# Top-k attention with a squared-ReLU layer on one core: the order of the last two batches, the place of the V casts, and the end of the program

## The chip, the core and the metric

One of the eight cores of a Trainium2 chip runs the whole program. The core has TensorE (PE in the profile, with its weight loads as PEld), VectorE (DVE), ScalarE (ACT), GpSimd (POOL) and SyncE (SP), each with an instruction queue of its own that it works off in order; waits between them go by semaphores. The metric is the device time of one execution in microseconds (us), and a kernel's time is the median of its runs.

## The reference

Attention over 8 batches of 8 heads, 576 rows of 64, in which each row keeps only its 32 largest scores; then a layer with a squared ReLU over the 4608 tokens.

```python
scores = scale * np.matmul(q, k.transpose(0, 1, 3, 2))
kth = np.partition(scores, -top_k, axis=-1)[..., -top_k:-top_k + 1]
scores = np.where(scores >= kth, scores, -1000000000.0)
attn = softmax(scores)                       # top_k = 32
x = np.matmul(attn, v)                       # tokens x 512, heads side by side
h = np.maximum(x @ w_in, 0.0)                # 512 -> 2048
out = h * h @ w_out                          # 2048 -> 512
```

## The kernel before

**Steps.** Two heads of a batch form a pair, so there are 32 pairs, four to a batch. A head's 576 rows are four chunks of 128 and a rest of 64. One step takes two blocks of 128 rows by 576 scores: chunk c of both heads of a pair, or the rests of two pairs. The list `steps` (L224 to L231) has 18 steps a batch, U = 144 in all, numbered u. In each batch the first pair does its four chunks, then come the rests of the first two pairs, then the other three pairs go chunk by chunk in turn, with the rests of the last two pairs behind chunk 0. A chunk of the tokens (`x_tok`) is complete when all four pairs have done it, so the four chunks of a batch are complete at its steps 7, 11, 14 and 17, counted from 0.

**One step on the engines.** TensorE makes the scores of step u+1 into two PSUM tiles, `sc_a` and `sc_b` (L254), and ScalarE copies them to `s` (L257). VectorE takes pairwise maxima (`pairs_of`, L273 and L274; `quads_of`, L282 and L283) and finds the 32 largest values in four rounds of MAX8 and MATCH_REPLACE8 (`topk`, L333 and L337). ScalarE's "far copy" (`copy_far`, L289) brings one half of the maxima from PSUM to `most`, which GpSimd (`lesser`, L307) and L282 of the next step read. ScalarE negates the ends of the top-k (`negate`, L352); GpSimd marks what is to be dropped (`drop`, L369), and a DMA with accumulation (L373) takes it off `s`. Two steps later ScalarE takes the exponentials (`exps`, L377) and SP starts a DMA transpose to `wT` (`turn`, L386). TensorE multiplies `wT` with V (`products`, `weigh`, L412) into `av`, one PSUM tile for all steps; VectorE inverts the sums (`invert`, L417) and ScalarE writes the scaled result into `x_tok` or, for rests, `x_rem` (`place`, L433 and L440). `finish` is `invert` and `place`. A step's products are taken `back` = 3 steps later and finished a step after that; from u = Z = U - 5 on `back` is 2.

**Preparing a pair.** `prep_units` has four parts: the transposes of q and of k (`main`, ScalarE's copy L162), those of the rests (`rest`, L199, L200, L202), and the casts of V (`values`, L206 and twice L209). `prepare` runs one part a step (two before step 8), between the exponentials and the far copy; `due` says when a pair is begun, and if a pair isn't ready when its scores are to be made, a loop ahead of `scores` runs what is missing. Its ten loads go three a step through SP's queue (`fetch`).

**The layer.** Two complete chunks (in the last batch one) make a block: `x_unit` turns them, with a DMA transpose (L477) or on TensorE (L470, the last batch's chunks 1 to 3, which wait in the list `moves`), and the rests of two batches make a block in the same way (`rem_unit`, L483, L489). A block is eight "up" pieces (four for one chunk with half the rows each: L514, then ReLU L519 and square L525 on ScalarE, or L523 on VectorE once `late` is set), and four "down" pieces a chunk (L537, over 16 matmuls in one PSUM bank `dn_ps`), then a copy (L542) and a store (L544). One chunk of 128 rows in the last batch is thus four up and four down pieces of about the same work. `piece` takes one from either list in turn; `dense(u, x)` runs, for x = 0 and x = 1, one piece each, or two each in the last 14 steps (L582), and filler matmuls (L553) if there is none. With `later`, what ScalarE does after a piece is put off to the next step (`behind`).

**The end.** Three blocks of the last two steps are masked on VectorE (L381) instead of being dropped by DMA, and the last two steps' weights are turned on TensorE (`turn_by_tensor`, L397, copies L399 and L401). Three more rounds of the loop, u = U to U + 2, do this together with products, pieces and `finish`; the pieces that are left follow in a last loop (L744). An up piece's PSUM tile is one of two `gen` buffers, in the last rounds sometimes `sc_a` or `sc_b` (L508). If a flag shows that the fast way did not separate the 32 largest values, a general version runs behind; it takes no part in the times here.

Of the kernel before, what the change touches and what calls it, by code (L numbers as in the profile page):

```python
# [23 lines left out]
def kernel(  # L24
# [192 lines left out]
    def whole(i):  # L217
        return [((i, c, 0), (i, c, 1)) for c in range(4)]
# [5 lines left out]
    steps = []  # L224
    for b in range(B):
        p0 = 4 * b
        steps += whole(p0) + rests(p0)
        for c in range(4):
            steps += [((i, c, 0), (i, c, 1)) for i in range(p0 + 1, p0 + 4)]
            if c == 0:  # L230
                steps += rests(p0 + 2)  # L231
    U = len(steps)
    first = {}
# [153 lines left out]
        st[u]["wT"] = wT  # L387


    def turn_by_tensor(u, x):  # L390
        if x == 0:
            st[u]["wT"] = scp.tile([128, 9, 128], bf16, name="wT", bufs=3)
            st[u]["tp"] = ps_sc.tile([128, 2, 1024], bf16, name="sc_" + "ab"[u - U + 2])
        flat = w_two[u % 3][:, :, :].rearrange("p x n -> p (x n)")
        tp = st[u]["tp"][:, x, 0:512 + 128 * x].rearrange("p (n r) -> p n r", r=128)
        for n in range(4 + x):
            pin(nc.tensor.transpose(tp[:, n, :], flat[:, (4 * x + n) * 128:(4 * x + n + 1) * 128], id_h[:, :]))  # L397
        if x == 0:
            pin(nc.vector.tensor_copy(st[u]["wT"][:, 0:4, :], tp))  # L399
        else:  # L400
            pin(nc.scalar.activation(st[u]["wT"][:, 4:9, :], tp, AF.Copy))  # L401

    def weigh(u, x):
        i, c, a = steps[u][x]
        va, wT = prep[i][3], st[u]["wT"]
        o = av[:, x, :]
        for g in range(2 if c == 4 else 1):
            rows = slice(64 * g, 64 * g + 64) if c == 4 else slice(0, 128)
            h = g if c == 4 else a
            for n in range(5):  # L410
                block_of, chunk = (5 * x + n, n) if n < 4 else (4, 4 + x)
                pin(nc.tensor.matmul(out=o[rows], lhsT=wT[:, block_of, rows], rhs=va[:, chunk, h, :], start=(n == 0), stop=(n == 4)))  # L412
        av_left[i] -= 1

    def invert(u):
        r = small.tile([128, 2, 1], f32, name="rsum", bufs=4)
        pin(nc.vector.reciprocal(r[:, :, :], av[:, :, 64:65]))  # L417
        st[u]["r"] = r

    x_tok = {}  # L420
# [4 lines left out]
    def place(u):  # L425
        for x, (i, c, a) in enumerate(steps[u]):
            b, pr = pairs[i]
            o, r = av[:, x, :], st[u]["r"]
            if c < 4:
                if (b, c) not in x_tok:  # L430
                    x_tok[b, c] = ffp.tile([128, 512], bf16, name="x_tok", bufs=8)
                h = 2 * pr + a
                pin(nc.scalar.activation(x_tok[b, c][:, h * 64:(h + 1) * 64], o[:, 0:64], AF.Copy, scale=r[:, x, :]))  # L433
# [63 lines left out]
    def block(xt, stores):  # L497
# [72 lines left out]
    def dense(u, x, later=False):  # L570
# [8 lines left out]
        if x == 1:  # L579
            moves.extend(soon_moves)  # L580
            soon_moves.clear()
        N = 2 if u >= U - 14 or len(ups) + len(downs) > 24 else 1  # L582
        for n in range(N):
            if not piece(later and N == 1) and n == 0 and u < U:
                idle_piece()
# [78 lines left out]
            x_unit(u, b, c)  # L664
        full.clear()

    for u in range(U + 3):
        back = 3 if u < Z else 2
        for x in range(2):
            if ok(u - 1) and u < U and not by_vector(u - 1, x):  # L670
                drop(u - 1, x)
        if ok(u):
            quads_of(u)
            topk(u, (0,))
# [9 lines left out]
        if ok(u - 2) and u < U:  # L684
            exps(u - 2, 0)
            exps(u - 2, 1)
            turn(u - 2)
        fetch(10 if u < 8 else 3)
        if u == U:
            late.append(True)  # L690
            mask(u - 2, 1)
            mask(u - 1, 0)
            mask(u - 1, 1)
        for _ in range(2 if u < 8 else 1):
            prepare(u)
        if u >= Z:
            turn_x(u)
        if ok(u):
            topk(u, (1, 2))
            if ok(u + 1):  # L700
                pairs_of(u + 1)
                copy_far(u + 1)
                lesser(u + 1)
            topk(u, (3,))
        if ok(u) and by_vector(u, 1):
            early_exps(u)
        if u == U - 1:
            exps(u - 1, 0)
        if u < U:
            dense(u, 0)  # L710
        if u < U:
# [6 lines left out]
        if u == U:  # L718
            turn_by_tensor(u - 2, 0)
            turn_by_tensor(u - 2, 1)  # L720
            dense(u, 0)
            products(u - 2)
            turn_by_tensor(u - 1, 0)
            turn_by_tensor(u - 1, 1)
            pin(nc.vector.tensor_reduce(worst[:, :], flags[:, :, :].rearrange("p f n -> p (f n)"), axis=mybir.AxisListType.X, op=ALU.max))
            pin(nc.vector.tensor_scalar(worst[:, :], worst[:, :], scalar1=0.0, scalar2=None, op0=ALU.is_gt))
            dense(u, 1)
        if u > U:
            products(u - 2)
            if u == U + 1:  # L730
                tail.append(0)
            dense(u, 1)
        turn_x(u)
        if w_casts and u >= 3:
            w_casts.pop(0)()
        if w_loads and u >= 1:
            w_loads.pop(0)()
    count = ps_one.tile([128, 512], f32, name="gen", bufs=2)
    pin(nc.tensor.matmul(out=count[0:1, 0:1], lhsT=worst[:, :], rhs=ones[:, :], start=True, stop=True))
    bad = const.tile([1, 1], mybir.dt.int32, name="bad")  # L740
# [135 lines left out]
```

## Time and profile before

| | us |
|---|---|
| median of 3 runs | 977.53 |
| lowest, highest | 976.54, 981.47 |
| the profiled execution, its own time | 976.03 |
| its span, first to last instruction | 974.2 |
| mean granted TensorE clock in it | 0.911 of full |

In the lists of the profile a group or a row reads: line, engine, operation, what is written <- what is read, the shapes, the count, and in brackets the idle time of the engine just before, with the instruction that ended it. A row of the timeline begins with its start and its duration in us; instructions overlap a little on one engine, so that the distance between two starts says what one costs in a row. A row of the stretches gives the length, then for each engine the busy time and the count, then the granted clock, the share of the DMA engines and GB/s. A row of the waits gives total us, times and the longest.

### The profile page before, as it was taken

How to read it: one execution, taken by the hardware profiler on the slowest of the kernel's cores; microseconds unless marked ns; L12 is line 12 of the kernel's file. 1: busy time of each engine (PE TensorE's matmuls, PEld its weight loads, DVE VectorE, ACT ScalarE, POOL GpSimd, SP SyncE). 2: the span in 40 equal slices, each digit the busy share in tenths (PEclk: the TensorE clock that was granted, in tenths of full speed). 3: DMA queues.
4: the chain of work that ended last, by engine and by line, in shares of the span. 5: the costliest groups of instructions: out<-in, count | busy, mean ns of one | idle time of the engine just before them, and what ended most of it. 6: DMA issues, size and time to landing. Idle time of an engine off the chain costs nothing.

```text
span 974.2 us, 19144 instructions
## 1 busy us (share of the span) xinstructions
PE 691.3 (71%) x5280; PEld 426.2 (44%) x5280; DVE 904.0 (93%) x3637; ACT 785.6 (81%) x1776; POOL 776.4 (80%) x803
## 2 busy tenths in 40 slices
PE   6766677786776786777677678676677667776756
PEld 3433344444444354444454345344454435443544
DVE  6999999999999999999999999999999999889741
ACT  4677797888888888888888879798898879776852
POOL 7888888888988888888888888878888888777520
PEclk9799988889999988989989988999989899998988
DMA  5576867889998998899997999998997899766421
GB/s 135 136 155 162 163 133 151 172 191 202 199 190 178 201 200 177 191 186 207 192 194 162 198 206 189 189 188 190 196 208 161 196 211 180 157 144 140 96 61 36
DMA packets 329969, 166.17 MB, mean 171 GB/s; under 512 B 306560, under 2 KB 306560, under 8 KB 329856
## 3 DMA queue, kind: packets, MB, share of 16 engines
q1 hardware_dynamic: 311088, 92.62, 48.8%
q0 software_dynamic: 17568, 71.97, 32.1%
q8 instruction: 45, 0.74, 0.3%
q14 instruction: 68, 0.56, 0.2%
q10 hardware_dynamic: 1200, 0.30, 0.1%
HBM read 37.75 MB, written 9.44 MB: 48 GB/s over the span
## 4 chain that ended last, share of the span: by engine, by line
DVE 50%; ACT 23%; issue 11%; PE 10%; DMA 5%; POOL 1%; SPq 1%; ACTq 0%; DVEq 0%; POOLq 0%
DVE m L333 20%; DVE cat L337 13%; ACT s L257 6%; DVE cat L282 4%; DVE cat L283 4%; DVE sc_b L273 4%; DVE most L274 3%; PE gen L514 3%; ACT w_two_b L377 2%; ACT w_two_a L377 2%; PE sc_a L254 2%; ACT rl L519 2%; PE dn_ps L537 2%; ACT w_two_c L377 2%; PE sc_b L254 1%
## 5 line engine op out<-in xcount | busy, mean ns | idle before, releaser
L333 DVE MAX8 m<-cat 128x8 f32<-128x104 f32 (+3 forms) x1152 | 445.3, 427 | 0.0
L337 DVE MATCH_REPLACE8 cat<-m,cat 128x104 f32<-128x104 f32 (+2 forms) x864 | 269.6, 319 | 0.0
L298 POOL TENSOR_TENSOR cat<-s 128x576 int32<-128x576 int32 (+1 forms) x144 | 224.1, 1556 | 15.2 <-ACT s L257 15.1
L307 POOL TENSOR_TENSOR cat<-cat,most 128x576 int32<-128x576 int32 (+1 forms) x144 | 190.3, 1322 | 50.2 <-ACT most L289 27.3
L254 PE MATMUL sc_b<-qkT 64*128 64x288 f32 x512 | 105.9, 489 | 113.2 <-DVE cat L283 74.7
L514 PE MATMUL gen<-xT,w_in 128*128 128x256 bf16 (+1 forms) x1104 | 147.5, 287 | 50.4 <-ACT qkT L162 22.5
L514 PEld LDWEIGHTS <-w_in 128*128 128x128 bf16 x1408 | 128.3, 106 | 102.2 <-issue 70.5
L537 PE MATMUL dn_ps<-w_out,h 128*128 128x512 bf16 x576 | 163.5, 421 | 5.4 <-ACT wide L542 5.4
L254 PE MATMUL sc_a<-qkT 64*128 64x288 f32 x512 | 104.7, 484 | 46.7 <-DVE most L274 32.4
L369 POOL TENSOR_SCALAR gone_b<-s,neg 128x576 uint8<-128x576 f32 x142 | 106.4, 749 | 24.2 <-ACT neg L352 13.0
L369 POOL TENSOR_SCALAR gone_a<-s,neg 128x576 uint8<-128x576 f32 x143 | 107.1, 749 | 21.2 <-ACT neg L352 9.9
L433 ACT ACTIVATE x_tok<-av_ps,rsum 128x64 bf16<-128x64 f32 x256 | 66.0, 309 | 71.0 <-DVE rsum L417 70.6
L254 PEld LDWEIGHTS sc_b<-qkT 64*128 64x128 f32 x512 | 49.8, 211 | 158.4 <-ACT rl L519 63.5
L257 ACT ACTIVATE s<-sc_b 128x576 f32<-128x576 f32 x144 | 94.6, 657 | 6.5 <-PE sc_b L254 6.1
L257 ACT ACTIVATE s<-sc_a 128x576 f32<-128x576 f32 x144 | 93.7, 651 | 6.8 <-PE sc_a L254 6.1
L519 ACT ACTIVATE rl<-gen 128x512 f32<-128x512 f32 x141 | 83.4, 591 | 12.9 <-PE gen L514 12.8
L525 ACT ACTIVATE h<-rl 128x512 bf16<-128x512 f32 x136 | 85.7, 630 | 4.3
L537 PEld LDWEIGHTS <-h 128*128 128x128 bf16 x576 | 55.7, 105 | 75.7 <-issue 37.9
L412 PEld LDWEIGHTS <-wT 128*128 128x128 bf16 (+1 forms) x1600 | 65.8, 104 | 52.3 <-DMA wT<-w_two_b 13.6
L273 DVE TENSOR_TENSOR sc_b<-sc_a,s 128x288 f32<-128x288 f32 x144 | 65.8, 457 | 8.6 <-ACT s L257 6.5
L282 DVE TENSOR_TENSOR cat<-sc_b,most 128x288 f32<-128x288 f32 x144 | 64.0, 444 | 7.0 <-ACT most L289 5.5
L373 POOL DMA_DIRECT2D s<-gone_b x61 | 54.2, 888 | 20.2 <-DVE m L333 13.9
(165 smaller groups left out, 1214.6 us busy)
## 6 DMA issues: line engine op xcount, KB each, us to landing
s<-gone_a POOLq DMA_DIRECT2D x61, 576.0 KB, 4.8
s<-gone_b POOLq DMA_DIRECT2D x61, 576.0 KB, 4.7
v_raw<-in_v_dram SPq DMA_DIRECT2D x64, 128.0 KB, 3.2
out_dram<-wide SPq DMA_DIRECT2D x32, 256.0 KB, 2.7
k_raw<-in_k_dram SPq DMA_DIRECT2D x63, 128.0 KB, 3.1
q_raw<-in_q_dram SPq DMA_DIRECT2D x63, 128.0 KB, 3.3
wide<-in_moe_w_in_dram SPq DMA_DIRECT2D x8, 512.0 KB, 4.4
wide<-in_moe_w_out_dram SPq DMA_DIRECT2D x8, 512.0 KB, 3.9
```

The costliest lines, as they stand in the source:

```text
L254: pin(nc.tensor.matmul(out=ps[j][:, x, 0:HALF], lhsT=lhsT, rhs=rhs, start=True, stop=True))
L257: pin(nc.scalar.activation(s[:, :, j * HALF:(j + 1) * HALF], ps[j][:, :, 0:HALF], AF.Copy))
L273: pin(tt(far, one[:, :, QUAR:HALF], two[:, :, QUAR:HALF], op=ALU.max))
L282: pin(tt(cat[:, :, 0:QUAR], far, near, op=ALU.max))
L298: pin(tt(less, s[:, :, 0:wide].bitcast(i32), s[:, :, HALF:HALF + wide].bitcast(i32), op=ALU.add))
L307: pin(tt(less, less, d["most"][:, 0:n_h, :, :].bitcast(i32).rearrange("p h x n -> p x h n"), op=ALU.subtract))
L333: pin(nc.vector.max(out=m[r][:, x, :], in_=part(r, x)))
L337: pin(nc.vector.match_replace(out=part(r, x), in_to_replace=m[r][:, x, :], in_values=part(r, x), imm_value=NEG))
L369: pin(nc.gpsimd.tensor_scalar(byte[:, x, :, 1], s[:, x, :], scalar1=d["neg"][:, x, 1:2], scalar2=-HUGE, op0=ALU.add, op1=ALU.mult))
L514: pin(nc.tensor.matmul(out=hp[:, n * n_rows:(n + 1) * n_rows], lhsT=w_in[:, kh, (f0 + n) * 128:(f0 + n + 1) * 128], rhs=xt(kh), start=(kh ...
L519: pin(nc.scalar.activation(rl[:, :], hp, AF.Relu))
L537: pin(nc.tensor.matmul(out=op[:, :], lhsT=held["h2"][:, f, c * 128:(c + 1) * 128], rhs=w_out[:, f, :], start=(f == 0), stop=(f == NF - 1)))
```

## The change

- `steps`: the last batch takes its chunks one by one, all four pairs for chunk 0 and chunk 1 within eight steps, then the rests of all pairs, then chunk 2, then chunk 3. Its chunks are complete at its steps 4, 7, 13 and 17. The batch ahead does two pairs whole before the other two go chunk by chunk; its chunks are complete at steps 10, 12, 15 and 17.
- `prepare`: when a pair's next part is the V casts, it comes behind the far copy and the last round of the top-k instead of ahead of them.
- `dense`: in the last 14 steps two pieces for x = 0 and one for x = 1, three instead of four, and what follows the third is put off to the next step up to step U - 2.
- `back` is gone: products are taken three steps later up to the last step.
- The three rounds behind the loop are written out as one sequence: masks first, then the finishing of step U - 4; the weights of step U - 2 are copied by ScalarE, those of U - 1 by VectorE; the sums of the last two steps have banks of their own in `sc_a` (`sums`) instead of `av`; `late` is set later, and of the last up pieces' PSUM tiles one in three is `sc_b`.

```diff
@@ steps @@
         p0 = 4 * b
+        if b == B - 1:
+            at = [((0, 0), (1, 0), (2, 0), (0, 1), (3, 0), (1, 1), (2, 1), (3, 1)), [(j, 2) for j in range(4)], [(j, 3) for j in range(4)]]
+            at = [[whole(p0 + j)[c] for j, c in some] for some in at]
+            steps += at[0] + rests(p0) + rests(p0 + 2) + at[1] + at[2]
+            continue
         steps += whole(p0) + rests(p0)
+        alone = 1
+        if b == B - 2:
+            steps += whole(p0 + 1)
+            alone = 2
         for c in range(4):
-            steps += [((i, c, 0), (i, c, 1)) for i in range(p0 + 1, p0 + 4)]
-            if c == 0:
+            steps += [whole(i)[c] for i in range(p0 + alone, p0 + 4)]
+            if c == alone - 1:
                 steps += rests(p0 + 2)
@@ turn_by_tensor @@
-    def turn_by_tensor(u, x):
+    def turn_by_tensor(u, x, by_scalar):
...
-        if x == 0:
-            pin(nc.vector.tensor_copy(st[u]["wT"][:, 0:4, :], tp))
+        to = st[u]["wT"][:, 4 * x:4 + 5 * x, :]
+        if by_scalar:
+            pin(nc.scalar.activation(to, tp, AF.Copy))
         else:
-            pin(nc.scalar.activation(st[u]["wT"][:, 4:9, :], tp, AF.Copy))
+            pin(nc.vector.tensor_copy(to, tp))
@@ weigh, invert, place: av becomes sums(u) @@
+    def sums(u):
+        if u < U - 2:
+            return av
+        if not last_two:
+            last_two["ps"] = ps_sc.tile([128, 2, 512], f32, name="sc_a")
+        return last_two["ps"][:, u - (U - 2), 0:130].rearrange("p (x d) -> p x d", x=2)
@@ up @@
-                if tail and tail[0] % 4 > 1:
-                    hp = ps_sc.tile([128, 2, 512], f32, name="sc_" + "ab"[tail[0] % 2])[:, 0, :]
+                if tail and tail[0] % 3 == 0:
+                    hp = ps_sc.tile([128, 2, 512], f32, name="sc_b")[:, 0, :]
@@ dense @@
-        N = 2 if u >= U - 14 or len(ups) + len(downs) > 24 else 1
+        N = 2 if (u >= U - 14 and x == 0) or len(ups) + len(downs) > 24 else 1
@@ the loop @@
-    for u in range(U + 3):
-        back = 3 if u < Z else 2
+    for u in range(U):
...
-        finish(u - 1 - back)
+        finish(u - 4)
...
-        for _ in range(2 if u < 8 else 1):
+        casts_next = bool(soon) and soon[0].__name__ == "values"
+        for _ in range(0 if casts_next else 2 if u < 8 else 1):
             prepare(u)
...
+        topk(u, (3,))
+        if casts_next:
+            prepare(u)
...
-            if u != Z - 1:
-                dense(u, 1, later=8 <= u < Z)
-            products(u - back)
-            if u == Z - 1:
-                finish(u - 3)
-                products(u - 2)
...
+        dense(u, 0)
+        dense(u, 1, later=8 <= u < U - 1)
+        products(u - 3)
@@ behind the loop @@
+    mask(U - 2, 1)
+    mask(U - 1, 0)
+    mask(U - 1, 1)
+    finish(U - 4)
+    turn_x(U)
+    turn_by_tensor(U - 2, 0, True)
+    turn_by_tensor(U - 2, 1, True)
+    turn_by_tensor(U - 1, 0, False)
+    dense(U, 0)
+    products(U - 3)
+    finish(U - 3)
+    turn_by_tensor(U - 1, 1, False)
+    products(U - 2)
+    turn_x(U)
+    dense(U, 1)
+    products(U - 1)
+    finish(U - 2)
+    finish(U - 1)
...
+    dense(U, 1)
+    turn_x(U)
+    late.append(True)
+    tail.append(0)
+    dense(U + 1, 1)
```

More of the change, by code (lines that the diff above doesn't have):

```diff
@@ L405, in weigh @@
         va, wT = prep[i][3], st[u]["wT"]
-        o = av[:, x, :]
+        o = sums(u)[:, x, :]
         for g in range(2 if c == 4 else 1):
@@ L413, in weigh @@
         av_left[i] -= 1
+    last_two = {}
+    def sums(u):
[4 more added lines that the diff above has]
+        return last_two["ps"][:, u - (U - 2), 0:130].rearrange("p (x d) -> p x d", x=2)
     def invert(u):
         r = small.tile([128, 2, 1], f32, name="rsum", bufs=4)
-        pin(nc.vector.reciprocal(r[:, :, :], av[:, :, 64:65]))
+        pin(nc.vector.reciprocal(r[:, :, :], sums(u)[:, :, 64:65]))
         st[u]["r"] = r
@@ L427, in place @@
             b, pr = pairs[i]
-            o, r = av[:, x, :], st[u]["r"]
+            o, r = sums(u)[:, x, :], st[u]["r"]
             if c < 4:
@@ L665, in turn_x @@
         full.clear()
-    for u in range(U + 3):
-        back = 3 if u < Z else 2
+    for u in range(U):
         for x in range(2):
-            if ok(u - 1) and u < U and not by_vector(u - 1, x):
+            if ok(u - 1) and not by_vector(u - 1, x):
                 drop(u - 1, x)
-        if ok(u):
-            quads_of(u)
-            topk(u, (0,))
+        quads_of(u)
+        topk(u, (0,))
         while behind:
             behind.pop(0)()
-        finish(u - 1 - back)
+        finish(u - 4)
         if ok(u + 1):
@@ L683 @@
             both(u + 1)
-        if ok(u - 2) and u < U:
+        if ok(u - 2):
             exps(u - 2, 0)
@@ L697 @@
             turn_x(u)
[L698 to L705, printed above, removed]
+        topk(u, (1, 2))
+        if ok(u + 1):
+            pairs_of(u + 1)
+            copy_far(u + 1)
+            lesser(u + 1)
+        topk(u, (3,))
+        if casts_next:
+            prepare(u)
+        if by_vector(u, 1):
             early_exps(u)
@@ L737 @@
             w_loads.pop(0)()
+    mask(U - 2, 1)
[16 more added lines that the diff above has]
+    finish(U - 1)
+    pin(nc.vector.tensor_reduce(worst[:, :], flags[:, :, :].rearrange("p f n -> p (f n)"), axis=mybir.AxisListType.X, op=ALU.max))
+    pin(nc.vector.tensor_scalar(worst[:, :], worst[:, :], scalar1=0.0, scalar2=None, op0=ALU.is_gt))
+    dense(U, 1)
[3 more added lines that the diff above has]
+    dense(U + 1, 1)
     count = ps_one.tile([128, 512], f32, name="gen", bufs=2)
```

23 lines of the change are left out of this document (removed).

## The prediction

> **What bounds the kernel now.** First the page: busy shares, then the busy tenths over the span.
>
> ```profile
> span 974.2 us, 19144 instructions
> PE 691.3 (71%) x5280; PEld 426.2 (44%) x5280; DVE 904.0 (93%) x3637; ACT 785.6 (81%) x1776; POOL 776.4 (80%) x803
> DVE  6999999999999999999999999999999999889741
> ```
>
> VectorE (DVE) is busy 93% of the span. The reader is to see where it is not: the first slice, two slices of 8, and the last four. The loop is VectorE's; the end is not. So the next view is the busy time by stretches, cut at the start of step 20, of step 127, of step 143, at the end of the last top-k instruction, and in the end.
>
> ```profile
> core 0: us, PE busy (x) PEld busy (x) DVE busy (x) ACT busy (x) POOL busy (x), PEclk, DMA share, GB/s
> 142.94:809.79 666.85, 477.19 (x3667) 297.53 (x3668) 657.91 (x2676) 575.30 (x1321) 567.48 (x555) 0.91 0.92 189
> 809.79:925.97 116.18, 86.23 (x711) 54.16 (x709) 99.48 (x403) 88.86 (x199) 83.58 (x81) 0.91 0.65 143
> 925.97:935.09 9.12, 4.78 (x40) 3.21 (x39) 5.54 (x24) 6.44 (x14) 4.14 (x4) 0.81 0.50 106
> 935.09:957.00 21.91, 13.26 (x134) 9.54 (x133) 6.76 (x14) 8.78 (x19) 0.95 (x3) 0.84 0.10 20
> 957.00:974.20 17.20, 11.85 (x116) 7.58 (x113) 3.46 (x5) 4.84 (x10) 0.00 (x0) 0.92 0.14 51
> ```
>
> An undisturbed step is measured between two L282 instructions, the first that VectorE does in a step:
>
> ```profile
> 299.07 0.46 DVE L282 TENSOR_TENSOR cat<-sc_b,most 128x288 f32<-128x288 f32 x1
> ...
> 303.13 0.46 DVE L273 TENSOR_TENSOR sc_b<-sc_a,s 128x288 f32<-128x288 f32 x1
> ...
> 305.19 0.44 DVE L282 TENSOR_TENSOR cat<-sc_b,most 128x288 f32<-128x288 f32 x1
> ```
>
> 6.12 us a step, and L273, which needs the score copies of ScalarE (ACT), starts 4.06 us into it. The second stretch holds 16 steps: 16 x 6.12 = 97.9, it took 116.18, so 18.3 us are lost there; step 143 adds 9.12 - 5.54 = 3.6. Together 21.9 us are lost in steps 127 to 143, and 39.1 us (935.09 to 974.2) pass after the last top-k. Who causes the loss, the waits of VectorE say, between 30 and 800 us (first row) and after 800 (second):
>
> ```profile
> DVE cat L282 <- ACT most L289: 4.0, 8, 0.7
> ...
> DVE rsum L417 <- PE av_ps L412: 19.3, 10, 3.6
> ```
>
> L417 waits for the sums of TensorE (PE): 19.3 us in ten waits at the end. One of them in the timeline, step 139:
>
> ```profile
> 890.12 1.44 ACT L377 ACTIVATE w_two_b<-s,neg 128x576 bf16<-128x576 f32 x2
> 891.59 1.30 SPq L386 DMA_TRANSPOSE wT<-w_two_b  x1
> 894.83 0.57 PEld L412 LDWEIGHTS <-wT 128*128 128x128 bf16 x10 [5.57 <-DMA wT<-w_two_b]
> 895.68 0.17 DVE L417 RECIPROCAL rsum<-av_ps 128x2 f32<-128x2 f32 x1 [1.81 <-PE av_ps L412]
> ```
>
> The exponentials end at 891.56, the transpose lands 3.2 us later, TensorE has stood still 5.57 us for it, and VectorE 1.81. Here the products are taken two steps back, so a transpose issued in a step is wanted in the same step.
>
> **The change part by part.**
>
> *Products three steps back to the end.* The transpose of step u-3 is issued in step u-1 and used in step u, one whole step (6.12 us) after, against the 3.2 us above. The five waits of steps 139 to 143 go, and their price is inside the 21.9.
>
> *Order of the last two batches, three pieces a step.* Counted from the instruction order of the two programs: before, steps 136 to 138 have only fillers for TensorE, chunk 0 of the last batch opens its block in step 139, and steps 130 to 134 and 139 to 143 carry up to four pieces, in steps 130, 134 four down pieces in a row over one PSUM bank. After, chunk 0 opens in step 136, chunk 1 in 138, steps 130 to 143 hold three pieces each, mostly up, down, up, and of the last thirty steps only 125 has fillers. The loads of each pair move with it on SP's queue, three a step; pair 31's last four are issued together in step 127, and what needs them stands in steps 128 and 129. So the long waits of steps 131, 133, 135 lose their cause too. I take all 21.9 away and set new costs against it.
>
> *ScalarE's new load.* One step of it, with the V casts (L206, L209) ahead of the far copy (L289), and, from another step, the first and the last of the three copies of a pair's rest:
>
> ```profile
> 309.71 0.21 ACT L199 ACTIVATE qbd_c<-gen 64x64 f32<-64x64 f32 x1
> ...
> 310.17 0.28 ACT L202 ACTIVATE qkT<-gen 128x128 f32<-128x128 f32 x1
> ...
> 503.31 0.63 ACT L206 ACTIVATE vau_b<-v_raw 128x512 bf16<-128x512 f32 x1
> 503.83 0.63 ACT L209 ACTIVATE vau_b<-v_raw 64x128 bf16<-64x128 f32 x2
> 504.49 0.41 ACT L289 ACTIVATE most<-sc_b 128x288 f32<-128x288 f32 x1
> 504.93 0.21 ACT L352 ACTIVATE neg<-m 128x4 f32<-128x4 f32 x1
> 505.04 0.58 ACT L519 ACTIVATE rl<-gen 128x512 f32<-128x512 f32 x1
> 505.65 0.63 ACT L525 ACTIVATE h<-rl 128x512 bf16<-128x512 f32 x1
> 506.67 0.52 ACT L433 ACTIVATE x_tok<-av_ps,rsum 128x64 bf16<-128x64 f32 x2 [0.39 <-DVE rsum L417]
> 507.08 0.65 ACT L257 ACTIVATE s<-sc_a 128x576 f32<-128x576 f32 x1
> ...
> 508.14 1.45 ACT L377 ACTIVATE w_two_b<-s,neg 128x576 bf16<-128x576 f32 x2
> ```
>
> From start to start: casts 1.2, negation 0.1, an up piece's two passes 1.2, placing 0.4, scores 1.1, exponentials 1.4, far copy 0.4, rest copies 0.65. The fixed part is 3.4, and two up pieces make 5.8 of 6.12: three pieces a step fit, without much room.
>
> In two steps they don't. The last batch uses a new pair in steps 126, 127, 128 and 130, so pair 30's rest and casts come in step 127 ahead of the scores, and pair 31's in step 129. Step 127: negation 0.1, the passes put off from step 126 (an up piece 1.2, the remainder's two copies 0.6, an estimate by L433's two in 0.52) to 1.9, placing 2.3, rest and casts 4.2, scores 5.3 against the 4.06 at which L273 wants them: 1.3 lost, and 0.2 more on the far copy behind the first q copy. Step 128 begins 1.2 late and loses 0.2. Step 129: 1.2 late, an up piece to 2.5, placing 2.9, rest and casts 4.8, scores 6.0: 1.9 lost. Sum 3.6, I take 4 (bounds 0, if the lateness is hidden, and 8, twice it, if the exponentials' transfers slip with it). Steps 131 to 143, counted the same way, lose 0.5.
>
> *The slow clock.* Eight down matmuls in step 130, and eight after a wait in step 131:
>
> ```profile
> 830.40 1.90 PE L537 MATMUL dn_ps<-w_out,h 128*128 128x512 bf16 x8
> 834.87 3.57 PE L537 MATMUL dn_ps<-w_out,h 128*128 128x512 bf16 x8 [2.56 <-ACT wide L542]
> ```
>
> After 2.56 us of standing the same work takes 1.7 us more. Steps 131 to 143 will have some such places still; I put three of them at 1 us each on the path: 3 us (0 to 9). The Trainium skill, in "TensorE: Matmul & The Clock Gate", section "Why this matters for your kernels", wants no TensorE gaps over about 3 us, else half the clock. The doubling agrees, the gap in this row is shorter than the page's. By the page alone, with pieces in every step, the 3 us would fall away and the sum would be 3 lower.
>
> *V casts behind the far copy.* All eight early waits of L282 for L289 (4.0 us) follow a step with V casts; the far copy at 504.49 above is one that came late. Three ScalarE instructions change places with one, and no transfer hangs on them. The casts still come before the next scores, so some of it returns at L273: I take 3.5 off (0 to 4.0). No other order changes before the last two batches.
>
> *The new tail.* Before, L417 stands ahead of the masks, and each piece's chain passes ScalarE and VectorE one at a time. From 957 on the pieces run at TensorE's pace:
>
> ```profile
> 960.82 1.06 PE L514 MATMUL gen<-xT,w_in 128*128 128x128 bf16 x16
> ...
> 962.58 1.06 PE L514 MATMUL gen<-xT,w_in 128*128 128x128 bf16 x16
> ...
> 968.88 0.60 ACT L542 ACTIVATE wide<-dn_ps 128x512 f32<-128x512 f32 x1 [2.86 <-PE dn_ps L537]
> ```
>
> From one up piece to the next, with a down piece between them, 1.76: 0.88 us a piece; 974.2 - 969.48 = 4.7 us from the last copy's end. Before, 20 pieces follow the last top-k, after it 22, since steps carry three and not four. After, counted from the last top-k: ScalarE comes 3.3 late out of step 143 (place, exponentials of two steps, two up pieces, one copy: 8.8 of 5.54), placing and the two transpose copies (0.7 and about 0.5, see L401 below) end at 4.9; TensorE: sums of 142 at 5.4, a down piece, sums of 143 at 6.8, an up piece 7.7; both sums now in banks of their own, so neither waits for the other's placing; placing ends at 8.0, chunk 3 is turned at 8.5, a down piece to 9.4. The other 17 pieces take 15.0, one wait on the single down bank where two blocks' down pieces meet 1.0: 25.4; copy 0.6, store 4.7: 30.7. With 1.5 for one slow stretch (as above): 32.2 instead of 39.1.
>
> ```profile
> L401 ACT ACTIVATE wT<-sc_a 128x640 bf16<-128x640 bf16 x1 | 0.7, 704 | 1.9 <-PE sc_a L397 1.9
> ```
>
> *Sum.* Last top-k: 935.1 - 21.9 - 3.5 + 4 + 0.5 + 3 = 917.2. End: 917.2 + 32.2 = 949.4. The profiled execution took 976.03 for a span of 974.2, so 1.8 lie around it: 951.2. It was 1.5 below the median of 977.53: **953**.
>
> **The rivals.**
>
> *The tail gains nothing* (12%): it is a chain of latencies, ScalarE is late into it, and two pieces more at 0.88 come on top: 39.1 + 1.8 = 40.9, that is 8.7 more: 961. For it: 21.9 us for nine pieces from 935 to 957. Against: a part of that is one bank shared by three steps' sums, and the transposes came behind pieces.
>
> *Half the loss stays* (17%): the cause was the clock, not the distance of two steps. Then 11 of the 21.9 remain where I set 3.5: 960. For it: granted clock 0.81 in step 143; against: the 5.57 us wait has a transfer's name on it.
>
> *ScalarE binds the last 17 steps, slower* (9%). Place: from step 127. A late negation delays the dropping on GpSimd, that the accumulating transfer, that the exponentials two steps on, behind which the next negation stands on the same engine. It decides once lateness outgrows the slack of that ring:
>
> ```profile
> 893.48 1.57 POOL L369 TENSOR_SCALAR gone_a<-s,neg 128x576 uint8<-128x576 f32 x2
> 895.36 0.89 POOL L373 DMA_DIRECT2D s<-gone_a  x1 [0.30 <-POOL gone_a L369]
> ...
> s<-gone_a POOLq DMA_DIRECT2D x61, 576.0 KB, 4.8
> ```
>
> 0.2 + 1.6 + 0.9 + 4.8 = 7.5 of the 12.2 us that two steps give; my count has ScalarE at most 3.3 late, under the 4.7 left. If it goes over, each step may last like the worst five of before, steps 139 to 143:
>
> ```profile
> 892.26 0.44 DVE L282 TENSOR_TENSOR cat<-sc_b,most 128x288 f32<-128x288 f32 x1
> ```
>
> from there to 935.09, 42.8 / 5 = 8.6. 17 x (8.6 - 6.12) = 42 in place of 7.5: 953 + 34 = 987.
>
> **How the numbers follow.** The forecast holds with 62%, its own range 944 to 960 from the bounds (casts 0 to 4, burst 0 to 8, clock 0 to 9, tail 30 to 36). To 965 the range takes in the two rivals that are still faster; the slower one is left out. Half a per cent, 4.9 us, is about what a measurement of this kernel can tell. Faster 0.88, the same 0.04, slower 0.08, the last nearly all from the third rival.
>
> **What would show it.** Right: L417's waits for the sums after 800 us fall from 19.3 below 6; L282's for L289 before 800 vanish; steps 131 to 143 near 6.4; two long steps, 127 and 129, ended by score copies; the last top-k near 917, the rest near 32. Wrong: L417 waiting still with the granted clock low (second rival), ScalarE without gaps from 127 and steps over 7 (third), more than 37 us after the last top-k (first).

## The result, and the profile after

| | before | after |
|---|---|---|
| median of 4 runs, us | 979.5 | 952.74 |
| lowest, highest | 976.54, 983.4 | 949.89, 954.23 |
| ratio, 95% interval | | 0.9721 [0.9675, 0.9767] |
| the profiled execution, its own time and span | 976.03, 974.2 | 953.31, 951.5 |

The change saves 2.8%. The page of the changed kernel: span, busy shares, and VectorE's busy tenths over the span.

```profile
span 951.5 us, 19120 instructions
PE 690.8 (73%) x5264; PEld 424.4 (45%) x5264; DVE 900.3 (95%) x3635; ACT 785.7 (83%) x1778; POOL 775.7 (82%) x803
DVE  5999999999999999999999999899999999899972
```

VectorE does nearly the same work as before (900.3 against 904.0 us). As before, two slices ahead of the end hold an 8, while the three thin ones at the end (7, 4, 1) have become two (7, 2). The busy time by stretches is cut at the same places as before: the start of step 20, of 127, of 143, the end of the last top-k, and one cut in the tail.

```profile
142.67:807.84 665.17, 481.74 (x3656) 298.66 (x3657) 656.40 (x2677) 571.90 (x1315) 566.24 (x555) 0.91 0.92 189
807.84:910.80 102.96, 80.11 (x688) 51.74 (x687) 98.17 (x402) 92.85 (x207) 85.16 (x82) 0.93 0.79 166
910.80:917.50 6.70, 4.90 (x38) 3.20 (x38) 5.52 (x25) 5.17 (x12) 2.49 (x3) 0.75 0.50 117
917.50:930.00 12.50, 8.94 (x135) 7.05 (x135) 5.34 (x12) 9.63 (x23) 2.34 (x3) 1.00 0.14 36
930.00:951.50 21.50, 14.57 (x133) 8.96 (x129) 4.16 (x6) 5.38 (x9) 0.00 (x0) 0.93 0.14 41
```

Steps 127 to 142 went from 116.18 to 102.96, which is 13.2 less; step 143 from 9.12 to 6.7 (2.4 less); the tail from 39.1 to 34.0 (5.1 less); steps 20 to 126 from 666.85 to 665.17 (1.7 less). With 0.3 ahead of step 20 that is the 22.7 between the spans. So the gain is where the prediction put it, at the end of the loop and in the tail. The waits of VectorE, first between 30 and 800 us, then after 800:

```profile
DVE rsum L436 <- PE av_ps L422: 3.8, 4, 2.2
DVE sc_b L282 <- ACT s L266: 2.7, 5, 1.1
DVE cat L291 <- ACT most L298: 1.7, 1, 1.7
...
DVE h L542 <- ACT rl L538: 7.8, 6, 2.5
DVE sc_b L282 <- ACT s L266: 4.0, 2, 2.5
DVE rsum L436 <- PE av_ps L422: 3.3, 3, 1.7
```

The lines have moved: L436 is the former L417, L422 the former L412, L291 the former L282, L282 the former L273, L266 and L298 the score and far copies. After 800 us the wait for the sums fell from 19.3 to 3.3. The largest that is new in the loop is 4.0 us for score copies, in two places; L542 stands in the tail. Before 800 us one wait for the far copy is left, of 1.7 us. The same spot of step 139 as shown of before:

```profile
885.56 1.39 SPq L395 DMA_TRANSPOSE wT<-w_two_b  x1
...
890.41 0.40 PEld L422 LDWEIGHTS <-wT 128*128 128x128 bf16 x10
890.46 0.47 PE L422 MATMUL av_ps<-vau_e,wT 128*128 128x65 bf16 x10
...
894.00 0.16 DVE L436 RECIPROCAL rsum<-av_ps 128x2 f32<-128x2 f32 x1
```

The transpose issued in step 138 is used in 139, 4.85 us on, and none of the three rows behind it carries a wait. The sums are inverted in step 140.

### The profile page after: what moved, and what is told of

Its sections match the earlier page's. It is cut to its first block, busy times and chain, and to the rows that moved or that the text cites. A ratio compares the mean times of both kernels' runs of the same rounds, so it can differ in the third digit from the quotient of the medians.

```text
span 951.5 us, 19120 instructions
## 1 busy us (share of the span) xinstructions
PE 690.8 (73%) x5264; PEld 424.4 (45%) x5264; DVE 900.3 (95%) x3635; ACT 785.7 (83%) x1778; POOL 775.7 (82%) x803
## 4 chain that ended last, share of the span: by engine, by line
DVE 61%; ACT 15%; issue 11%; PE 7%; DMA 3%; SPq 1%; POOL 1%; ACTq 0%; POOLq 0%
DVE m L342 25%; DVE cat L346 16%; DVE sc_b L282 5%; ACT s L266 5%; DVE cat L291 5%; DVE cat L292 5%; DVE most L283 4%; ACT w_two_b L386 2%; PE gen L533 2%; ACT w_two_a L386 2%; PE dn_ps L556 1%; PE sc_a L263 1%; DVE rsum L436 1%; PE sc_b L263 1%; ACT x_tok L452 1%
## 5 line engine op out<-in xcount | busy, mean ns | idle before, releaser
L307 POOL TENSOR_TENSOR cat<-s 128x576 int32<-128x576 int32 (+1 forms) x144 | 218.6, 1518 | 17.9 <-ACT s L266 17.0
L263 PE MATMUL sc_b<-qkT 64*128 64x288 f32 x512 | 109.1, 495 | 118.8 <-DVE cat L292 55.9
L266 ACT ACTIVATE s<-sc_b 128x576 f32<-128x576 f32 x144 | 94.7, 657 | 7.5 <-PE sc_b L263 7.3
L266 ACT ACTIVATE s<-sc_a 128x576 f32<-128x576 f32 x144 | 93.7, 651 | 5.1 <-PE sc_a L263 4.4
L422 PEld LDWEIGHTS <-wT 128*128 128x128 bf16 (+1 forms) x1600 | 66.4, 105 | 33.1 <-DMA wT<-w_two_c 7.4
L282 DVE TENSOR_TENSOR sc_b<-sc_a,s 128x288 f32<-128x288 f32 x144 | 66.3, 461 | 12.0 <-ACT s L266 9.9
L263 PEld LDWEIGHTS sc_a<-qkT 64*128 64x128 f32 x512 | 44.8, 197 | 65.4 <-ACT w_two_c L386 16.3
L386 ACT ACTIVATE w_two_a<-s,neg 128x576 bf16<-128x576 f32 x96 | 69.6, 783 | 1.8 <-DMA s<-gone_a 1.6
```

The costliest lines, as they stand in the source:

```text
L263: pin(nc.tensor.matmul(out=ps[j][:, x, 0:HALF], lhsT=lhsT, rhs=rhs, start=True, stop=True))
L266: pin(nc.scalar.activation(s[:, :, j * HALF:(j + 1) * HALF], ps[j][:, :, 0:HALF], AF.Copy))
L282: pin(tt(far, one[:, :, QUAR:HALF], two[:, :, QUAR:HALF], op=ALU.max))
L307: pin(tt(less, s[:, :, 0:wide].bitcast(i32), s[:, :, HALF:HALF + wide].bitcast(i32), op=ALU.add))
L386: pin(nc.scalar.activation(w_two[u % 3][:, x, 0:S], d["s"][:, x, :], AF.Exp, bias=d["neg"][:, x, 0:1]))
```

## The experiments

All on the same kind of chip, each beside runs of the kernel before. "Last top-k" and "tail" (from it to the end) come from the profiled execution, whose span stands beside them; "127 to 142" are those 16 steps.

| kernel | median (lowest, highest) | ratio [interval] | span | 127 to 142 | last top-k | tail |
|---|---|---|---|---|---|---|
| m_back | 959.88 (958.46, 962.34) | 0.9824 [0.9777, 0.9871] | 959.5 | 110.05 | 925.35 | 34.2 |
| b_only | 969.27 (966.39, 973.1) | 0.9895 [0.9855, 0.9934] | 964.6 | 110.96 | 924.90 | 39.7 |
| m_order | 955.47 (951.91, 962.74) | 0.9805 [0.9742, 0.9868] | 950.1 | 103.75 | 913.33 | 36.8 |
| o_only | 968.82 (964.56, 975.37) | 0.9908 [0.9878, 0.9938] | 965.3 | 119.38 | 934.73 | 30.6 |
| m_three | 953.2 (952.74, 954.55) | 0.976 [0.9716, 0.9803] | 951.5 | 112.12 | 922.54 | 29.0 |
| m_casts | 955.5 (951.89, 961.52) | 0.9801 [0.9745, 0.9857] | 950.1 | 103.46 | 916.46 | 33.6 |
| m_sums | 957.4 (955.84, 960.26) | 0.9774 [0.974, 0.9809] | 954.9 | 103.01 | 918.46 | 36.4 |
| n_early | 956.57 (955.39, 960.44) | 0.977 [0.9734, 0.9805] | 953.6 | 100.32 | 919.88 | 33.7 |
| n_both | 959.19 (956.23, 961.14) | 0.9787 [0.9752, 0.9822] | 956.8 | 99.85 | 924.70 | 32.1 |
| after_again | 953.7 (950.26, 955.92) | 0.9752 [0.9715, 0.9788] | 950.9 | 102.79 | 914.43 | 36.5 |
| n_shift | 949.88 (948.15, 950.95) | 0.9714 [0.968, 0.9747] | 946.3 | 98.80 | 912.64 | 33.7 |
| n_best | 946.69 (945.21, 949.93) | 0.9685 [0.9649, 0.9721] | 945.1 | 98.66 | 912.15 | 33.0 |

Those of one batch share a chip and the runs of before: m_back, m_order, m_three, m_casts (before 976.6); n_early, n_both, b_only, m_sums (978.85); the other four (979.0). after_again is the changed kernel without an edit.

### The distance: m_back and b_only

m_back is the changed kernel with products two steps back in the last five steps; b_only is the kernel before with nothing but three steps back to the end; the products and the finish of the third step from the end then open the tail.

```diff
 # m_back
+        back = 3 if u < Z else 2
...
-        products(u - 3)
+        products(u - back)
+        if u == Z - 1:
+            finish(u - 3)
+            products(u - 2)
...
 # b_only
-        back = 3 if u < Z else 2
+        back = 3 if u <= U else 2
...
```

> The changed kernel with one part undone: in the last five steps the products are again taken two steps back instead of three (order, three pieces, V casts and the tail stay). Theory (distance): each of steps 139 to 143 waits again for a transpose issued in the same step, about 2 us a step, so the sums' waits of VectorE in these steps are 8 to 12 us, the last top-k instruction ends near 927 instead of 917.5, and the time is 960 to 964. Rival (load and slow clock made the waits of before, not the distance): under 3 us of such waits, time 952 to 956.

> The kernel before with one part of the change alone: products three steps back up to the last step, the tail only so far adapted that the third step's products and finish are added at its start. Theory: the waits for the sums in steps 139 to 143 (11.7 us) go, those of steps 131, 133 and 135 (5 us, four down pieces over one bank, late clock) stay, and the tail gets one step's products more, 1 to 3 us: 966 to 970. Rival (four pieces a step alone make the waits): 973 to 978.

m_back in the timeline, at step 139:

```profile
886.52 1.39 SPq L395 DMA_TRANSPOSE wT<-w_two_b  x1
...
890.29 0.57 PEld L422 LDWEIGHTS <-wT 128*128 128x128 bf16 x10 [4.43 <-DMA wT<-w_two_b]
...
891.13 0.17 DVE L436 RECIPROCAL rsum<-av_ps 128x2 f32<-128x2 f32 x1 [2.33 <-PE av_ps L422]
```

With one step less of distance the wait is back, under a transfer's name and at 4.43 us, though order, pieces and tail are the new ones. Steps 139 to 142 take 8.84, 7.60, 7.70 and 7.59 instead of 6.1 to 6.3, and the last top-k comes 7.8 later. The other way round, b_only takes 10.2 off the last top-k (935.09 to 924.90) and leaves the waits of steps 131 to 136 and 140, which another part has to take. In both, about 1.5 of this lies in steps 20 to 126, which the edit does not touch. Steps 127 to 143 alone are 6.8 longer in m_back and 8.7 shorter in b_only, so the distance is shown as a cause from both sides, worth 7 to 9 us. The clock follows the distance here: in step 139 it was 0.61 in m_back and 1.00 in the changed kernel, and no run says how much of a wait is the transfer's and how much the slow pace behind it. The waits for sums in m_back add up to 7.1 us, slightly less than expected.

### The order and the pieces: m_order, o_only, m_three

m_order is the changed kernel with the old list of steps, o_only the kernel before with the new list. m_three has four pieces a step at the end:

```diff
-        N = 2 if (u >= U - 14 and x == 0) or len(ups) + len(downs) > 24 else 1
+        N = 2 if u >= U - 14 or len(ups) + len(downs) > 24 else 1
```

> The changed kernel with the old order of the steps in the last two batches (three pieces, products three back, V casts and new tail stay). Theory: the bursts of steps 127 and 129 (4.8 us in the profile of the changed kernel) go, since the pairs come spread out; against that chunk 0 opens its block only in step 139, fillers come back in 137 and 138, and 25 instead of 22 pieces follow the last top-k, 3 x 0.88 = 2.6 us: the time is 950 to 955, so the order by itself gains little or nothing. Rival (the order carries the gain): the late blocks cost as before, 960 or more.

> The kernel before with the new order of the steps alone (products two steps back from step 139 on, four pieces, V casts ahead, old tail). Theory: the order brings the burst of steps 127 and 129 (4.8 us) and leaves the waits for the sums of the last five steps; it gives 14 instead of 20 pieces after the last top-k, 6 x 0.88 = 5 us: 972 to 978, no gain that can be measured. Rival (the order is what saves): 965 or less.

> The changed kernel with four pieces a step in the last 14 steps instead of three. Theory: runs of four up or four down pieces in steps 130, 133 to 137, 141 and 142 bring back waits for the sums of 1 to 2.5 us each, 6 to 10 us by the last top-k; but 14 instead of 22 pieces follow it, 8 x 0.88 = 7 us less: the time is 951 to 957. Rival (four pieces cost nothing when the products have three steps): the time is 945 to 948, better than with three.

o_only by stretches, steps 127 to 142 and the tail:

```profile
807.43:926.81 119.38, 94.94 (x750) 62.64 (x749) 99.15 (x403) 95.55 (x213) 84.54 (x82) 0.83 0.67 146
934.73:965.30 30.57, 17.35 (x170) 11.40 (x170) 8.24 (x16) 11.46 (x24) 0.94 (x3) 0.88 0.15 39
```

The order alone gains 10.2 us by the medians, and nearly all of it in the tail: 30.57 instead of 39.1, with 14 pieces behind the last top-k in its trace instead of 21, while steps 127 to 142 got no shorter (119.38 against 116.18). Both my expectation and its rival missed here. Put on the other parts the order brings far less: m_order's 16 steps are 0.8 longer than the changed kernel's and its tail 2.8, and its median is 2 to 3 us higher, in ranges that overlap. The bursts went only in part: step 127 takes 6.13 us in it, 128 and 129 take 6.74 and 7.57. The parts don't add up; that with one part the other has less left to take is a reading that no run tests. m_three by stretches, and its step 139:

```profile
804.96:917.08 112.12, 88.40 (x764) 58.85 (x769) 98.90 (x402) 95.94 (x214) 83.58 (x81) 0.94 0.72 153
922.54:951.50 28.96, 19.18 (x222) 14.83 (x223) 8.15 (x15) 13.76 (x30) 2.34 (x3) 0.85 0.12 32
```

```profile
888.55 3.28 PE L533 MATMUL gen<-xT,w_in 128*128 128x128 bf16 x32 [3.61 <-ACT xT L490]
...
892.37 0.17 DVE L436 RECIPROCAL rsum<-av_ps 128x2 f32<-128x2 f32 x1 [2.40 <-PE av_ps L422]
```

Two up pieces in a row, behind a wait for the turned chunk, hold up the products and so VectorE. Four pieces a step cost 9.2 us in the 16 steps, and 5.0 come back in the tail, which has fewer pieces left. Most of the rest, 3.6, comes from steps 20 to 126, which this edit does not touch, and is chance of this execution; 1.3 comes from step 143, and 0.7 is lost again ahead of step 20. The medians cannot be told apart (953.2 against 952.74 and 953.7): three instead of four is mainly a trade, and these runs show no gain by it.

### The V casts: m_casts

```diff
-        for _ in range(0 if casts_next else 2 if u < 8 else 1):
+        for _ in range(2 if u < 8 else 1):
...
-        if casts_next:
-            prepare(u)
```

> The changed kernel with the V casts ahead of the far copy again. Theory: the waits of VectorE's first instruction of a step for the far copy come back, 4 us in eight places; the step near 590 us that waited for an accumulating transfer may or may not: the time is 954 to 958, and steps 20 to 126 take 667 to 669 us in the profile instead of 665. Rival (the lateness comes back at the score copies in any case): 951 to 954, steps 20 to 126 unchanged.

The waits of VectorE in m_casts, 30 to 800 us:

```profile
DVE cat L291 <- ACT most L298: 3.3, 6, 0.8
```

The waits for the far copy return, 3.3 us in six, and yet steps 20 to 126 take 664.8, against 665.2 in the changed kernel. The changed kernel loses time at other places instead: more in the waits for score copies (2.7 against 1.9), and two long steps, 92 and 93, of 8.28 and 7.42. A step 93 of over 7 us stands in five of the ten profiles with the casts behind and in none of the four with the casts ahead; that the move brings it is not shown. The median, 955.5, is 2 to 3 us above the changed kernel's, in ranges that overlap. Over all kernels of this study, the mean of steps 20 to 126 is 664.4 with the casts behind (eight profiles without extra loads, 661.6 to 667.3) and 665.4 with the casts ahead (four, 664.5 to 666.9). That is 1 us within a spread of almost 6: by these profiles the casts are worth about 1 us, and zero is not excluded.

### The tail: m_sums

```diff
     def sums(u):
-        if u < U - 2:
-            return av
...
+        return av
...
```

> The changed kernel with the sums of the last two steps in the one tile av again, each finished before the next step's products. Theory: TensorE waits twice for an inversion and a placing, about 1 us each, ahead of the last step's sums: 1 to 2.5 us more, 954 to 956. Rival (pieces fill the wait, or ScalarE's lateness covers it): 952 to 953.5.

With one bank for all sums, TensorE waits for the placing of the step before, in the timeline of m_sums:

```profile
926.81 0.46 PE L422 MATMUL av_ps<-vau_a,wT 128*128 128x65 bf16 x10 [1.17 <-ACT x_tok L448]
929.23 0.46 PE L422 MATMUL av_ps<-vau_b,wT 128*128 128x65 bf16 x10 [1.09 <-ACT x_tok L448]
```

These are 2.3 us. The last copy ends 30.5 us after the last top-k instead of 28.4, at the same granted clock of 1.00 in the first 12.5 us, so the waits lengthen the tail by about as much as they last. The median is higher than expected; in the profiled execution steps 20 to 126 took 667.3.

### The two long steps: n_early, n_both, n_shift, n_best

n_early makes two parts a step and issues ten loads at once in steps 121 to 126, so that the new pairs are ready in time. n_shift begins the last eight pairs four steps sooner and leaves loads and parts at their pace. n_best and n_both take n_shift and n_early, and issue both halves' transposes in the tail ahead of their copies.

```diff
 # n_early
-        fetch(10 if u < 8 else 3)
+        fetch(10 if u < 8 or 121 <= u < 127 else 3)
...
 # n_shift
     def due(i):
-        return first[4 * (i // 4) + 3] - 1 - 4 * (3 - i % 4) if i >= 4 else first[i] - 1
+        sooner = 4 if i >= NP - 8 else 0
+        return first[4 * (i // 4) + 3] - 1 - 4 * (3 - i % 4) - sooner if i >= 4 else first[i] - 1
 # n_best, n_both: turn_by_tensor returns its copy
+    halves = [turn_by_tensor(U - 2, 0, True), turn_by_tensor(U - 2, 1, True)]
+    for go in halves:
+        go()
...
```

> The changed kernel with the pairs of the last batch prepared earlier: two parts a step in steps 121 to 126 (V casts still behind the far copy) and all ten loads of a pair issued in one step there. Theory (the burst is what steps 127 and 129 lose): both fall from 8.86 and 8.25 us to 6.1 to 6.4, and steps 121 to 126, which hold down pieces or fillers and leave ScalarE room, grow by less than 1 us together: last top-k 4 to 5 us earlier, time 947 to 949.5. Rival (ScalarE is full in the whole stretch, so the work costs the same elsewhere, or the loads in a bunch stall TensorE): 951 to 954.

> As the run before it (pairs prepared earlier), and in the tail the transposes of both halves of step U-2, and of U-1, stand ahead of the copies of the halves instead of alternating with them. Theory (the tail is a chain of latencies on TensorE's queue, 1.7 us of it the second half's transposes waiting for the first half's copy): 1 to 1.5 us less than that run, 946 to 948.5. Rival (ScalarE, late out of step 143, sets the pace): no difference from that run.

> The changed kernel with the last eight pairs due four steps sooner, so that each pair is still prepared one part a step, with its loads three a step, and pairs 30 and 31 are ready before they are needed. Theory (the burst ahead of the scores, not ScalarE's sum, costs steps 127 and 129): both fall to 6.1 to 6.5 us, 4 to 5 us less than the changed kernel beside it: 946 to 949. Rival (ScalarE is full there): no more than 1 us less.

> The run before it, and in the tail the transposes of both halves ahead of the copies. Theory: 1.5 to 2 us less after the last top-k (32.1 us in the earlier run with this tail, 34.0 in the changed kernel), 944 to 947, below both given kernels. Rival: no difference from the run before it.

> The changed kernel once more, as the measure for the three runs beside it. Theory: 950 to 955, and its parts in the profile as the first time: 6.1 us a step from 131 on, 8 to 9 us in steps 127 and 129, about 34 us after the last top-k. If the stalls near steps 57, 92 and 93 (accumulating transfers that land late) are chance, steps 20 to 126 differ by some us from the 665.2 of the first profile.

n_early missed. Steps 127 to 142 did get shorter (100.32), but steps 123 to 126 took 11.78, 7.61, 7.69 and 7.15. Its timeline says why: SP issues the loads one behind the other, about 0.65 us each (the row covers two), and the step's own transposes of q and k wait for them.

```profile
782.01 1.28 SPq L104 DMA_DIRECT2D k_raw<-in_k_dram  x2
783.87 1.08 PE L161 MATMUL gen<-id_f,q_raw 128*128 128x128 f32 x4 [3.41 <-DMA q_raw<-in_q_dram]
788.32 1.09 PE L161 MATMUL gen<-id_f,k_raw 128*128 128x128 f32 x4 [3.37 <-DMA k_raw<-in_k_dram]
```

n_both repeats that (steps 123 and 125: 11.33 and 10.89) and missed too, with 959.19; its tail is 1.6 shorter than n_early's. n_shift does it without a stall. Its stretches, and the starts of steps 127, 129 and 130 in its timeline:

```profile
807.79:906.59 98.80, 74.41 (x678) 47.69 (x677) 98.08 (x402) 89.56 (x199) 85.39 (x82) 0.98 0.78 164
912.64:946.30 33.66, 23.51 (x264) 16.00 (x263) 9.47 (x18) 14.98 (x32) 2.34 (x3) 0.98 0.14 39
```

```profile
807.79 0.44 DVE L291 TENSOR_TENSOR cat<-sc_b,most 128x288 f32<-128x288 f32 x1
...
820.34 0.44 DVE L291 TENSOR_TENSOR cat<-sc_b,most 128x288 f32<-128x288 f32 x1
...
826.86 0.44 DVE L291 TENSOR_TENSOR cat<-sc_b,most 128x288 f32<-128x288 f32 x1
```

Steps 127 and 129 are 6.44 and 6.52 (826.86 - 820.34) instead of 8.86 and 8.25, and the 16 steps hold 98.80, where 16 undisturbed ones would take 97.9. By the medians n_shift is 3.8 us below after_again, a little less than expected, and their ranges overlap a little. n_best adds the tail's order. Two rows of its timeline, and the last copy, in n_shift and then in n_best:

```profile
914.23 0.66 PE L406 MATMUL sc_a<-id_h,w_two_b 128*128 128x128 bf16 x9
914.73 0.67 PE L406 MATMUL sc_b<-id_h,w_two_c 128*128 128x128 bf16 x9
```

```profile
940.40 0.60 ACT L561 ACTIVATE wide<-dn_ps 128x512 f32<-128x512 f32 x1 [3.70 <-PE dn_ps L556]
```

```profile
938.09 0.60 ACT L563 ACTIVATE wide<-dn_ps 128x512 f32<-128x512 f32 x1 [3.70 <-PE dn_ps L558]
```

The transposes no longer wait for a copy. The last copy ends 2.3 sooner than in n_shift, 0.5 of it from the last top-k and 1.8 from here. The span shows 1.2, since the store behind the copy took 6.4 us and not 5.3. Over all profiles that store takes 4.6 to 6.4 us and blurs the tails in the table; up to the last copy, n_early and n_shift take 28.36 us like the changed kernel, n_both and n_best 26.5. All six runs of n_best lie below all six of after_again, 7.0 us by the medians: it is faster than both given kernels, about 3.2% below the one before.

## Why the prediction was right

The mechanism was right in its main step, the distance, and the sizes of four smaller terms were off. The median came out at 952.74 where 953 was predicted, the last top-k at 917.5 for 917.2, the tail at 34.0 for 32.2. Step by step:

- **The loss of steps 127 to 143 (21.9 to go).** It went, with a distance of three steps and three pieces a step: steps 127 to 143 lose 6.2 us now, and the new costs below make up about that. Its cause was the distance (m_back, b_only, 7 to 9 us), and beside it the number of pieces (m_three, 9.2 in the 16 steps). That the new order shortens these steps is not shown: o_only's are not shorter, m_order's 0.8 longer. The rival in which half the loss stays by the clock falls, since m_back brings the waits back by an edit of the distance alone.
- **Two long steps, 127 and 129 (4).** They lost 2.7 and 2.1, 4.9 in all. Step 127:

```profile
811.12 0.28 ACT L202 ACTIVATE qkT<-gen 128x128 f32<-128x128 f32 x1
811.29 0.62 ACT L206 ACTIVATE vau_a<-v_raw 128x512 bf16<-128x512 f32 x1
811.45 0.85 PE L263 MATMUL sc_a<-qkT 64*128 64x288 f32 x1 [0.73 <-ACT qkT L202]
...
813.77 0.65 ACT L266 ACTIVATE s<-sc_b 128x576 f32<-128x576 f32 x1 [0.25 <-PE sc_b L263]
...
814.45 0.47 DVE L282 TENSOR_TENSOR sc_b<-sc_a,s 128x288 f32<-128x288 f32 x1 [2.49 <-ACT s L266]
```

  The late score copies are the predicted mechanism. What the count had left out is that TensorE's scores themselves wait for the copy of the pair's rest (L202), so that the second score tile is ready only at 813.7 and ScalarE waits too. In step 129 the same wait is 1.53, and step 128 lost nothing here (in after_again the three steps take 8.09, 7.47 and 7.51). The count also lacks a wait of 2.09 us of TensorE in step 128 for k of pair 31, whose load SP issued behind a late transpose; how much of step 129 is its, no run separates. n_shift takes both losses away.
- **Steps 131 to 143 (0.5).** This was about right: steps 138 and 139 took 0.2 more each, 6.32; the ten others up to 142 lie between 6.09 and 6.13.
- **The slow clock (3, of 0 to 9).** This term was too large. Only step 143 lost 1.2, at a granted clock of 0.75. There TensorE had stood 2.87 us for the copy out of the down bank, and four down matmuls behind it took 1.86 us instead of 1.03; what is the wait's and what the pace's is not separated. Step 140, the first of these two rows by stretches, had 0.72 and lost nothing:

```profile
892.48:898.61 6.13, 5.18 (x33) 3.22 (x34) 6.13 (x27) 6.07 (x14) 5.37 (x6) 0.72 0.73 176
898.61:904.70 6.09, 5.52 (x69) 3.81 (x67) 6.09 (x26) 5.72 (x14) 5.54 (x6) 1.00 0.75 160
```

  Its first down piece ran at half pace (1.89 instead of 1.03, shown at the end), and VectorE was busy for all 6.13 us. By the program, what absorbs it is the distance: sums that come late in a step are inverted only in the next one. By the row of the page "TensorE: Matmul & The Clock Gate" of the Trainium skill (section "Why this matters for your kernels") (no gaps of TensorE over some 3 us, else half the clock) this term would have been 0. That is nearer to the 1.2 than the 3 was, but the trace does not bear out the reason: no gap of TensorE in steps 131 to 143 is longer than 2.87 us, and the clock fell all the same, as the 0.72 shows.
- **The V casts (3.5, of 0 to 4).** Too large as well: about 1 by the profiles, with zero not excluded (m_casts). The waits for the far copy behind V casts went, as forecast; the one of 1.7 us that is left has another cause, shown below. But steps 20 to 126 became 1.7 us shorter and not 3.5: up to 800 us the waits for score copies grew from 2.0 to 2.7 us and those for the sums from 2.5 to 3.8. The step that failed is the size of "some of it returns at L273": more was lost again, and not at L273 alone. Which of these waits the move causes is open.
- **The tail (32.2).** The two sums in banks of their own were right (m_sums, 2.3), and so was the pace of 0.88 a piece. The last copy ended 28.4 after the last top-k, where the count has 26.0 (25.4 + 0.6), and the store behind it took 5.6 instead of 4.7. Of the 2.4 ahead of the copy, 1.7 is that the second half's transposes waited for ScalarE's copy of the first half out of the same tile. Three rows of the changed kernel, then one of the kernel before:

```profile
918.41 1.05 PE L533 MATMUL gen<-xt_rem_b,w_in 128*128 128x128 bf16 x16 [2.36 <-ACT rl L538]
...
921.71 0.44 PE L406 MATMUL sc_a<-id_h,w_two_b 128*128 128x128 bf16 x5 [1.71 <-ACT wT L409]
...
945.29 0.60 ACT L561 ACTIVATE wide<-dn_ps 128x512 f32<-128x512 f32 x1 [3.70 <-PE dn_ps L556]
```

```profile
940.50 0.52 PE L397 MATMUL sc_a<-id_h,w_two_b 128*128 128x128 bf16 x5 [2.95 <-DVE wT L399]
```

  The first is the late ScalarE that was counted. The second was not in the count, although the last row shows the same wait, 2.95 us long, in the kernel before; n_best, which also moves the second half of the last step forward, shows that it is worth 1.8. The 1.5 kept for one slow stretch was not needed here and made up for part of the rest. In after_again, where TensorE had a granted clock of 0.56 for 4 us of the tail, that stretch came: the last copy ended after 30.5, and the tail took 36.5.

```profile
919.00:923.00 4.00, 3.92 (x30) 2.79 (x30) 0.42 (x1) 0.74 (x2) 0.00 (x0) 0.56 0.00 0
```

- **The rivals.** The tail gained 5.1 and not nothing. ScalarE's score copies ended the long waits of steps 127 and 129 and of no others, so its slower case did not come.

The time is nearer than the terms were, and that is luck, twice. Up to the last top-k the slow clock cost 1.8 less than forecast, the long steps 0.9 more, and the steps ahead of 127 saved 2.0 instead of 3.5, which nearly cancels. Then the tail was 1.8 longer, so that the profiled execution took 953.31 where the working has 951.2. The working added 1.5, because the profile of before lay that much below its median; the profile of the changed kernel lies 0.6 above its median, and this took the 2.1 away again.

What stays open: why steps 20 to 126 differ by up to 5.7 us between profiles, with stalls near steps 57, 92 and 93 in some and not in others. In step 92 of the changed kernel the exponentials waited for an accumulating transfer, and the far copy behind them came late:

```profile
595.35 1.44 ACT L386 ACTIVATE w_two_a<-s,neg 128x576 bf16<-128x576 f32 x2 [1.61 <-DMA s<-gone_a]
597.60 0.46 DVE L291 TENSOR_TENSOR cat<-sc_b,most 128x288 f32<-128x288 f32 x1 [1.68 <-ACT most L298]
```

No run tried what delays the transfer. Nor were the other changes of the tail undone one by one (masks first, who makes the copies, the later `late`, `sc_b` in one of three); beyond the sums, its gain is not divided among them.

## What to carry to other kernels

Give the result of a transfer a whole step between issue and use when the transfer takes half of one: it was worth 7 to 9 us here, and with it a step at a granted clock of 0.72 lost nothing. When an order moves work forward, move the start of its preparation forward with it, at the old pace of loads (n_shift), not by loading faster (n_early). And before a change of pieces per step is called a gain, add what it takes from the tail to what it puts into the loop (m_three). Compare tails by the end of the last copy, not by the span, when the last store varies.

## What was not expected of the hardware

- Half pace came after a short gap. In step 140 of the changed kernel the down matmuls that follow a wait of 1.29 us run at half pace, while step 139 has a wait of the same 1.29 at the same place (ahead of the second score tile) and keeps full pace. Steps 131, 132, 136, 137, 138 and 142 have this wait too, at a granted clock of 1.00.

```profile
887.11 0.76 PE L263 MATMUL sc_b<-qkT 64*128 64x288 f32 x4 [1.29 <-ACT h L544]
888.71 1.03 PE L556 MATMUL dn_ps<-w_out,h 128*128 128x512 bf16 x4
...
893.43 0.79 PE L263 MATMUL sc_b<-qkT 64*128 64x288 f32 x4 [1.29 <-ACT h L544]
894.14 1.89 PE L556 MATMUL dn_ps<-w_out,h 128*128 128x512 bf16 x4
```

  So the length of the last gap alone does not decide it, and no run here says what does.
